# Second layer of a fused attention and two-layer kernel: y loaded a block earlier and split in place, weight conversion spaced out, weight sums kept, low parts on VectorE

## The chip, the cores and the metric

One core of a Trainium2 chip runs the whole program. The metric is device microseconds of one execution; "before" is the median of three runs. All trace numbers are from one profiled execution of the kernel before, in microseconds from its first instruction.

## What is computed

```python
# attention between x [8, 8, 512, 64] and state [8, 8, 32, 64], both ways,
# gives x of the next layer: 8 * 544 rows, 512 columns
gate = 1.0 / (1.0 + np.exp(-(x @ w_gate)))      # 512 -> 1536
y = gate * (x @ w_val) @ w_out                  # 1536 -> 512
h = y @ w_in                                    # 512 -> 2048
g = np.where(h >= 1, h, np.where(h <= -1, 0.0, (h + 1) ** 2 / 4.0))
out = g @ w_out2                                # 2048 -> 512
```

All in fp32. The kernel gets that accuracy from a faster matmul format (fp32r) by splitting every operand into a high and a low part and multiplying three times: high by high, high by low, low by high. The high part is a ScalarE copy, the low part a subtraction, raw minus high.

## The kernel before

The program is written as one order by hand: each engine executes its instructions in the order in which the code issues them, and every load and store is issued by SyncE, in that same order. The 4352 rows are nine blocks: eight (j = 0 to 7) of 512 rows, and a last one (j = 8) of 256 rows. The first layer writes its result y, block by block, to DRAM (`y_dram`).

**The block loop of the second layer's first product** (lines 1202 to 1234) has eight units per block, `n = 8 * j + m`. `emit_g2` (line 770) does one unit: 24 matmuls of 128 x 512 (`mm3`, lines 216 to 218; half as wide in the last block) into one of four PSUM tiles, then the activation in three steps: VectorE line 782, ScalarE line 785, VectorE line 786, into a tile `sg2` of three buffers. The store of that tile to `hd_dram` (line 787) is issued after the next unit has been emitted (`put`). The operand y of the next block is loaded after unit 6 of the current block by `load_y` (line 754) into two staging tiles, and split (`split`, lines 128 and 129: ScalarE y_hi, VectorE y_lo) before unit 7 is emitted. y_hi and y_lo have one tile in each of two pools, which the blocks use in turn.

Beside this, in units 0 to 23, weights are converted. `weights.slot` (line 191) advances a pipeline: load a row block of weights as raw words (`wraw`, line 146), two ScalarE steps (lines 155, 156), two VectorE steps (lines 162, 166), and then either a split (the last six tiles of w_in) or a store of the tile `ca` to `w2_dram` (line 176, 16 tiles of the second w_out). There are three buffers of `wraw` and of `ca`. The loop calls three slots in each of units 0 to 2, and two in each unit after.

**The last product** (`second`, line 865) multiplies in blocks of 2 x 2 by Strassen's scheme: seven products M1 to M7 instead of eight. Each of 36 groups of 14 steps needs seven h tiles (`hc`): `prep_h` loads four pieces of h, VectorE makes four sums (line 835), ScalarE the high parts (line 838), and the low parts (line 842) are made by VectorE and GpSimd in turn, four and three. A step is six matmuls of 256 columns, three in the last block (lines 794 to 796). The eight weight steps (w2 tiles, 0 to 7) are made by `prep_w2` (line 702): four loads from `w2_dram`, four sums on VectorE (line 727), high parts on ScalarE (735), low parts on VectorE (128 x 768) and GpSimd (128 x 1024; line 740). Steps 0 to 2 are prepared during the block loop, 3 to 7 during the first block of the last product, by a list of step numbers (`extra`):

```python
    for i in range(3, 8):
        load, *rest = prep_w2(i, w2p)
        if i < 5:
            load()
        else:
            extra.setdefault(7 * (i - 4), []).append(load)
        for n, f in enumerate(rest):
            extra.setdefault(7 * (i - 3) + n, []).append(f)
```

At the end of each block `combine` adds the seven products (line 924) and stores the output.

Of the kernel before, what the change touches and what calls it, by code (L numbers as in the profile page):

```python
# [25 lines left out]
def attention_moe_moe_kernel(  # L26
# [675 lines left out]
    def prep_w2(i, p):  # L702

        box = []

        def load():
            t = p.tile([128, 2, 7, 256], F32R, tag="w2", name="w2")
            x = wt_pool.tile([128, 256], F32, tag="wb", name="wb", bufs=2)
            box.extend((t, x))
            u = 4 * (i // 2) + i % 2  # L710
            a, b = w2_dram[u], w2_dram[u + 2]
            lo, hi = slice(0, 256), slice(256, 512)
            for n, d, c in ((0, a, lo), (1, b, lo), (2, b, hi), (None, a, hi)):
                nc.sync.dma_start(out=x if n is None else f32(t[:, 1, n]), in_=d[:, c])

        def sums():
# [4 lines left out]
            for o, a, b in (  # L721
# [5 lines left out]
                nc.vector.tensor_tensor(out=x[:, o - 3], in0=a, in1=b, op=SUB)  # L727
# [9 lines left out]
        def low(o, eng):  # L737
            src, n = part(o)
            t = box[0]
            eng.tensor_tensor(out=t[:, 1, n], in0=src, in1=f32(t[:, 0, n]), op=SUB)  # L740

        def last():
            low(False, nc.gpsimd)
            w2_t[i] = box[0]

        return [
            load,
            sums,
            lambda: high(True),
            lambda: (low(True, nc.vector), high(False)),  # L750
# [3 lines left out]
    def load_y(p, j, i, rp):  # L754
        n = S if j < B else NSB
        tag, bufs = ("hraw", 2) if rp is hr else ("io", 2)
        rv = rp.tile([128, 2, 512], F32, tag=tag, name="raw", bufs=bufs)[:, :, :n]
        nc.sync.dma_start(out=rv, in_=y_dram[j][:, 2 * i : 2 * i + 2])
        if i == 0:
            y_t[j] = (  # L760
                p.tile([128, 4, S], F32R, tag="y_hi", name="y_hi"),
                p.tile([128, 4, S], F32R, tag="y_lo", name="y_lo"),
            )
        hi, lo = y_t[j]
        o = slice(2 * i, 2 * i + 2)
        return lambda: split(hi[:, o, :n], lo[:, o, :n], rv)
# [3 lines left out]
    def emit_g2(j, m2):  # L770
# [10 lines left out]
        sg = p2.tile([128, 2, 512], F32, tag="sg2", name="sg2", bufs=3)[:, :, :n]  # L781
# [21 lines left out]
    def prep_h(q):  # L803
# [36 lines left out]
        def low(j, i):  # L840
            hi, lo = get(j)
            (nc.gpsimd if i % 2 else nc.vector).tensor_tensor(  # L842
                out=lo, in0=raw(j), in1=f32(hi), op=SUB
            )
# [441 lines left out]
```

## Time and profile before

| | us |
|---|---|
| three runs, median (lowest to highest) | 1592.81 (1589.39 to 1597.24) |
| the profiled execution | 1589.33 |
| its span, first to last instruction | 1587.2 |
| mean granted clock of TensorE, as a share of full speed | 0.969 |

The span is what the trace covers; 2.1 us of the execution's own time lie around it. In the trace, PE is TensorE, DVE is VectorE, ACT is ScalarE, POOL is GpSimd and SP is SyncE. L and a number is the line of the kernel above. Durations of neighbouring instructions on one engine overlap a little, since an instruction's end is counted when its write has been acknowledged.

### The profile page before, as it was taken

To read this page: it belongs to the slowest core of one execution; us is meant where nothing else is said; L and a number is where in the kernel's file an instruction comes from. 1 tells how busy PE (TensorE), PEld (TensorE's weight loads), DVE (VectorE), ACT (ScalarE), POOL (GpSimd) and SP (SyncE) were. 2 spreads that over 40 slices of the span, in tenths; PEclk is the share of its full clock that TensorE was granted. 3 is DMA by queue.
4 is the path that set the end of the run, shared out by engine and by line. 5 is a ranking of instruction groups with operands and counts; after the bars stand their busy time and mean duration, and the time that the engine had idled before them with its cause. 6 is when DMAs were issued, how large, how long until landed. Compare 5 with 4: busy or idle time off the path is not lost.

```text
span 1587.2 us, 28914 instructions
## 1 busy us (share of the span) xinstructions
PE 1469.1 (93%) x12176; PEld 1255.5 (79%) x12176; DVE 960.8 (61%) x1084; ACT 634.3 (40%) x896; POOL 223.2 (14%) x142
## 2 busy tenths in 40 slices
PE   7999978999899999999993999899998799999997
PEld 6677766887677777788972788677887799999997
DVE  6666455553466633441274645554455999999995
ACT  6655345433465523331253322222223444444442
POOL 2100022000000000000000000000002555545552
PEclk9999988999999999999996999999999899999999
DMA  6244455634466635754476532332345244444432
GB/s 212 95 161 168 154 207 191 200 120 153 162 230 235 232 124 195 236 198 146 145 232 224 187 117 109 132 121 106 120 146 167 72 134 134 133 134 134 133 121 80
DMA packets 140553, 249.86 MB, mean 157 GB/s; under 512 B 14729, under 2 KB 83337, under 8 KB 140425
## 3 DMA queue, kind: packets, MB, share of 16 engines
q1 hardware_dynamic: 140424, 248.03, 46.3%
q8 instruction: 95, 1.56, 0.4%
q14 instruction: 34, 0.27, 0.1%
HBM read 152.57 MB, written 95.42 MB: 156 GB/s over the span
## 4 chain that ended last, share of the span: by engine, by line
PE 70%; DVE 11%; DMA 9%; ACT 4%; issue 3%; SPq 1%; DVEq 0%; ACTq 0%
PE ps L510 17%; PE o L796 6%; PE o L794 6%; PE o L795 6%; PE ps L217 5%; PE ps L218 5%; PE ps L216 5%; PE ps L599 5%; PE ps L600 5%; PE ps L601 4%; DMA raw<-y_dram 3%; PE ps L483 3%; DMA w_dram<-ca 2%; ACT sg L785 2%; DVE cy L162 1%
## 5 line engine op out<-in xcount | busy, mean ns | idle before, releaser
L796 PE MATMUL o<-w,hc 128*128 128x256 f32 x952 | 271.1, 285 | 16.2 <-DVE hc L842 16.1
L794 PE MATMUL o<-w,hc 128*128 128x256 f32 x952 | 270.3, 284 | 2.4 <-DVE sg L786 1.7
L795 PE MATMUL o<-w,hc 128*128 128x256 f32 x952 | 269.8, 283 | 0.0
L510 PE MATMUL ps<-at_hi,M 32*128 32x512 f32 x3072 | 259.0, 398 | 3.0 <-ACT e L317 2.4
L216 PE MATMUL ps<-y_hi,wi 128*128 128x512 f32 (+1 forms) x576 | 221.3, 384 | 37.1 <-ACT y_hi L128 37.1
L217 PE MATMUL ps<-y_lo,wi 128*128 128x512 f32 (+1 forms) x576 | 221.9, 385 | 5.4 <-DVE y_lo L129 5.4
L218 PE MATMUL ps<-y_hi,wi 128*128 128x512 f32 (+1 forms) x576 | 220.6, 383 | 0.0
L796 PEld LDWEIGHTS o<-w,hc 128*128 128x128 f32 x952 | 183.2, 192 | 18.2 <-DVE hc L842 18.2
L510 PEld LDWEIGHTS ps<-at_hi,M 32*128 32x128 f32 x3072 | 151.8, 184 | 47.4 <-issue 15.3
L794 PEld LDWEIGHTS o<-w,hc 128*128 128x128 f32 x952 | 184.1, 193 | 3.3 <-issue 1.7
L795 PEld LDWEIGHTS o<-w,hc 128*128 128x128 f32 x952 | 183.1, 192 | 0.0
L785 ACT ACTIVATE sg<-sg,half 128x1024 f32<-128x1024 f32 (+1 forms) x72 | 79.6, 1105 | 233.9 <-DVE sg L782 233.9
L599 PE MATMUL ps<-oh_hi,wo 128*128 128x512 f32 x384 | 158.0, 411 | 4.0 <-ACT oh_hi L583 4.0
L600 PE MATMUL ps<-oh_lo,wo 128*128 128x512 f32 x384 | 154.0, 401 | 8.0 <-DVE oh_lo L585 7.9
L216 PEld LDWEIGHTS ps<-y_hi,wi 128*128 128x128 f32 x576 | 110.6, 192 | 59.7 <-ACT y_hi L128 38.8
L601 PE MATMUL ps<-oh_hi,wo 128*128 128x512 f32 x384 | 153.4, 400 | 3.7 <-DVE wo L187 3.7
L510 PE MATMUL ps<-at_lo,M 32*128 32x512 f32 x1536 | 156.8, 392 | 0.0
L842 POOL TENSOR_TENSOR hc<-hc 128x512 fp32r<-128x512 f32 (+1 forms) x72 | 112.0, 1555 | 301.9 <-ACT hc L838 186.7
L786 DVE TENSOR_TENSOR sg<-sg,ps 128x1024 f32<-128x1024 f32 (+1 forms) x72 | 83.7, 1162 | 96.9 <-ACT sg L785 96.9
L842 DVE TENSOR_TENSOR hc<-hs,hc 128x512 fp32r<-128x512 f32 (+1 forms) x108 | 139.4, 1332 | 0.0
L740 POOL TENSOR_TENSOR w<-wt,w 128x1024 fp32r<-128x1024 f32 x8 | 19.6, 2449 | 810.6 <-ACT w L735 810.6
L217 PEld LDWEIGHTS ps<-y_lo,wi 128*128 128x128 f32 x576 | 110.5, 192 | 28.9 <-DVE y_lo L129 8.3
(118 smaller groups left out, 2319.6 us busy)
## 6 DMA issues: line engine op xcount, KB each, us to landing
hd_dram<-sg SPq DMA_DIRECT2D x64, 512.0 KB, 2.9
h_dram<-sg SPq DMA_DIRECT2D x48, 512.0 KB, 4.4
hraw<-h_dram SPq DMA_DIRECT2D x48, 512.0 KB, 4.8
hc<-hd_dram SPq DMA_DIRECT2D x96, 256.0 KB, 4.1
wraw<-in_moe_w_out_dram SPq DMA_DIRECT2D x28, 512.0 KB, 4.0
wraw<-in_moe_w_gate_dram SPq DMA_DIRECT2D x48, 256.0 KB, 2.9
wraw<-in_moe_w_val_dram SPq DMA_DIRECT2D x48, 256.0 KB, 3.6
ws_dram<-w SPq DMA_DIRECT2D x24, 512.0 KB, 5.2
```

What stands on the lines that cost most here:

```text
L216: nc.tensor.matmul(out=ps, lhsT=wh, rhs=vh, start=(i == 0), stop=False)
L217: nc.tensor.matmul(out=ps, lhsT=wh, rhs=vl, start=False, stop=False)
L218: nc.tensor.matmul(out=ps, lhsT=wl, rhs=vh, start=False, stop=(i == n - 1))
L510: nc.tensor.matmul(out=ps[r // 2][:, r % 2], lhsT=M[o, l, e, c], rhs=a[o, e], start=(h == 0 and j == 0), stop=(h == H - 1 and j == 2),)
L599: nc.tensor.matmul(out=ps, lhsT=wh[:, c], rhs=hi, start=first, stop=False)
L600: nc.tensor.matmul(out=ps, lhsT=wh[:, c], rhs=lo, start=False, stop=False)
L601: nc.tensor.matmul(out=ps, lhsT=wl[:, c], rhs=hi, start=False, stop=last)
L785: nc.scalar.activation(out=sg, in_=sg, func=AF.Square, bias=half, scale=0.5)
L794: nc.tensor.matmul(out=ps, lhsT=wh, rhs=vh, start=start and i == 0, stop=False)
L795: nc.tensor.matmul(out=ps, lhsT=wh, rhs=vl, start=False, stop=False)
L796: nc.tensor.matmul(out=ps, lhsT=wl, rhs=vh, start=False, stop=last)
L842: (nc.gpsimd if i % 2 else nc.vector).tensor_tensor(out=lo, in0=raw(j), in1=f32(hi), op=SUB)
```

## The change

- y: `load_y` now makes both loads at once, straight into the memory of y_lo, and splits in place. The next block's y is loaded before unit 1 of the current block, and split before units 4 and 5. The staging tiles are gone, and `sg2` has two buffers instead of three.
- Conversion: from unit 3 on one slot per unit, to unit 27 instead of 23.
- Weights: four steps (0 to 3) are prepared in the block loop and stay resident. For steps 4 to 7 the four sums are also made there and kept in DRAM (`ws2_dram`); the last stage loads them (`ready`) and only splits.
- Low parts: all on VectorE, of the weights and of h.

```diff
@@ -699,32 +699,44 @@
...
-    def prep_w2(i, p):
+    ws2_dram = {i: tc.dram_tile([128, 4, 256], F32, name=f"ws2_dram_{i}") for i in range(4, 8)}
+    def prep_w2(i, p, kept=False, ready=False):
...
-            x = wt_pool.tile([128, 256], F32, tag="wb", name="wb", bufs=2)
...
-            for n, d, c in ((0, a, lo), (1, b, lo), (2, b, hi), (None, a, hi)):
-                nc.sync.dma_start(out=x if n is None else f32(t[:, 1, n]), in_=d[:, c])
+            box.append(t)
+            for n, src in enumerate((a[:, c], b[:, c], b[:, d])):
+                nc.sync.dma_start(out=f32(t[:, 1, n]), in_=src)
+            if ready:
+                box.append(f32(t[:, 1, 3:7]))
+                nc.sync.dma_start(out=box[1], in_=ws2_dram[i])
+            else:
+                x = wt_pool.tile([128, 256], F32, tag="wb", name="wb", bufs=2)
+                box.append(x)
+                nc.sync.dma_start(out=x, in_=a[:, d])
...
+        def keep():
+            nc.sync.dma_start(out=ws2_dram[i], in_=box[1])
...
@@ -734,36 +746,38 @@
...
-        def low(o, eng):
+        def low(o):
             src, n = part(o)
             t = box[0]
-            eng.tensor_tensor(out=t[:, 1, n], in0=src, in1=f32(t[:, 0, n]), op=SUB)
+            nc.vector.tensor_tensor(out=t[:, 1, n], in0=src, in1=f32(t[:, 0, n]), op=SUB)
         def last():
-            low(False, nc.gpsimd)
+            low(False)
             w2_t[i] = box[0]
-        return [
-            load,
-            sums,
+        if kept:
+            return [load, sums, keep]
+        return [load] + [sums] * (not ready) + [
             lambda: high(True),
-            lambda: (low(True, nc.vector), high(False)),
+            lambda: (low(True), high(False)),
             last,
         ]
...
-    def load_y(p, j, i, rp):
+    def load_y(p, j):
         n = S if j < B else NSB
-        tag, bufs = ("hraw", 2) if rp is hr else ("io", 2)
-        rv = rp.tile([128, 2, 512], F32, tag=tag, name="raw", bufs=bufs)[:, :, :n]
-        nc.sync.dma_start(out=rv, in_=y_dram[j][:, 2 * i : 2 * i + 2])
-        if i == 0:
-            y_t[j] = (
-                p.tile([128, 4, S], F32R, tag="y_hi", name="y_hi"),
-                p.tile([128, 4, S], F32R, tag="y_lo", name="y_lo"),
-            )
-        hi, lo = y_t[j]
-        o = slice(2 * i, 2 * i + 2)
-        return lambda: split(hi[:, o, :n], lo[:, o, :n], rv)
...
+        hi, lo = y_t[j] = (
+            p.tile([128, 4, S], F32R, tag="y_hi", name="y_hi"),
+            p.tile([128, 4, S], F32R, tag="y_lo", name="y_lo"),
+        )
+        def step(i):
+            o = slice(2 * i, 2 * i + 2)
+            raw = f32(lo[:, o, :n])
+            nc.sync.dma_start(out=raw, in_=y_dram[j][:, o])
+            return lambda: split(hi[:, o, :n], lo[:, o, :n], raw)
+        return [step(i) for i in range(2)]
...
@@ -778,7 +792,7 @@
...
-        sg = p2.tile([128, 2, 512], F32, tag="sg2", name="sg2", bufs=3)[:, :, :n]
+        sg = p2.tile([128, 2, 512], F32, tag="sg2", name="sg2", bufs=2)[:, :, :n]
...
-        def low(j, i):
+        def low(j):
             hi, lo = get(j)
-            (nc.gpsimd if i % 2 else nc.vector).tensor_tensor(
-                out=lo, in0=raw(j), in1=f32(hi), op=SUB
-            )
+            nc.vector.tensor_tensor(out=lo, in0=raw(j), in1=f32(hi), op=SUB)
...
@@ -1180,7 +1192,7 @@
...
-            ys = [load_y(pa, 0, c, hr) for c in range(2)]
+            ys = load_y(pa, 0)
...
@@ -1202,24 +1214,28 @@
...
-            if m == 7:
-                while ys:
-                    ys.pop(0)()
+            if m == 1 and j < B:
+                ys = load_y(yb if j % 2 == 0 else pa, j + 1)
+            if m in (4, 5) and j < B:
+                ys.pop(0)()
             then = emit_g2(j, m)
             if put:
                 put()
             put = then
-            if n < 24 and not weights.empty():
-                for _ in range(3 if n < 3 else 2):
+            if n < 28 and not weights.empty():
+                for _ in range(3 if n < 3 else 1):
                     weights.slot()
-            if n == 24:
+            if n == 28:
                 assert weights.empty()
                 st_conv.close()
-                w2p = pool("w2a", side="right", bufs=3)
+                w2p = pool("w2a", side="right", bufs=4)
                 wt_pool = pool("wt", side="right")
-                todo2 += [f for i in range(3) for f in prep_w2(i, w2p)]
+                todo2 += [f for i in range(4, 8) for f in prep_w2(i, w2p, kept=True)]
+                todo2 += [f for i in range(4) for f in prep_w2(i, w2p)]
             elif todo2 and n < 8 * B - 8:
-                todo2.pop(0)()
+                for f in todo2[: 2 if n % 3 == 0 else 1]:
+                    f()
+                del todo2[: 2 if n % 3 == 0 else 1]
...
-            if m == 6 and j < B:
-                ys = [load_y(yb if j % 2 == 0 else pa, j + 1, c, p2) for c in range(2)]
...
@@ -1238,19 +1252,19 @@
...
-    w2p = pool("w2b", stack=st_o, bufs=5)
+    w2p = pool("w2b", stack=st_o, bufs=4)
...
-    for i in range(3, 8):
-        load, *rest = prep_w2(i, w2p)
-        if i < 5:
+    for i in range(4, 8):
+        load, *rest = prep_w2(i, w2p, ready=True)
+        if i < 6:
             load()
         else:
-            extra.setdefault(7 * (i - 4), []).append(load)
+            extra.setdefault(7 * (i - 5), []).append(load)
         for n, f in enumerate(rest):
-            extra.setdefault(7 * (i - 3) + n, []).append(f)
+            extra.setdefault(7 * (i - 4) + 4 + n, []).append(f)
```

What the two orders look like at three places follows.

SyncE in block 0. Before, the second y (`y_dram_108`) is loaded here, behind unit 5's result (`hd_dram_116` is block 0's result, `w_dram_...` the converted rows of the second w_out, `ca` their source):

```order
L787 DMA hd_dram_116<-sg_9994 128x1024
L146 DMA wraw<-in_moe_w_out_dram 128x1024
L176 DMA w_dram_131<-ca 128x512
L146 DMA wraw<-in_moe_w_out_dram 128x1024
L176 DMA w_dram_132<-ca 128x512
L758 DMA raw<-y_dram_108 128x1024 x2
L787 DMA hd_dram_116<-sg_10042 128x1024
```

Now, from the block's first weight loads on:

```order
L146 DMA wraw<-in_moe_w_in_dram 128x4x256 x4
L777 DMA y_lo<-y_dram_108 128x1024 x2
L801 DMA hd_dram_116<-sg_9721 128x1024
L146 DMA wraw<-in_moe_w_in_dram 128x4x256 x2
L146 DMA wraw<-in_moe_w_out_dram 128x1024
L801 DMA hd_dram_116<-sg_9772 128x1024
L146 DMA wraw<-in_moe_w_out_dram 128x1024 x3
L801 DMA hd_dram_116<-sg_9838 128x1024
L146 DMA wraw<-in_moe_w_out_dram 128x1024
L176 DMA w_dram_125<-ca 128x512
L801 DMA hd_dram_116<-sg_9904 128x1024
```

The load has moved ahead of the block's first result and of all stores of `ca`, and there is one load and one store of weight rows per unit where there were two.

VectorE at the start of the last stage, before (`hs` are sums of h tiles, `hc` low parts, `wt` sums of weights, `w_...` low parts of weights), from the last activation step on:

```order
L786 TENSOR_TENSOR sg_12233<-sg_12233,ps_12208 128x2x256
L727 TENSOR_TENSOR wt<-wb,w_12257 128x256
L727 TENSOR_TENSOR wt<-w_12257,wt 128x256
L727 TENSOR_TENSOR wt<-w_12257,wb 128x256
L727 TENSOR_TENSOR wt<-w_12257,wt 128x256
L835 TENSOR_TENSOR hs_12293<-ht,hc 128x512
L835 TENSOR_TENSOR hs_12303<-hs_12293,hc 128x512
L835 TENSOR_TENSOR hs_12305<-hc,ht 128x512
L740 TENSOR_TENSOR w_12257<-w_12257 128x768
L835 TENSOR_TENSOR hs_12316<-hc,hs_12303 128x512
L842 TENSOR_TENSOR hc<-hc 128x512
L842 TENSOR_TENSOR hc<-hs_12303,hc 128x512
```

and now:

```order
L800 TENSOR_TENSOR sg_12282<-sg_12282,ps_12257 128x2x256
L849 TENSOR_TENSOR hs_12335<-ht,hc 128x512
L849 TENSOR_TENSOR hs_12344<-hs_12335,hc 128x512
L849 TENSOR_TENSOR hs_12346<-hc,ht 128x512
L849 TENSOR_TENSOR hs_12355<-hc,hs_12344 128x512
L856 TENSOR_TENSOR hc<-hc 128x512 x2
L752 TENSOR_TENSOR w_12306<-w_12306 128x768
L856 TENSOR_TENSOR hc<-hs_12344,hc 128x512
L752 TENSOR_TENSOR w_12306<-w_12306 128x1024
L856 TENSOR_TENSOR hc<-hc 128x512
```

The weight sums are gone, the weight's first low part stands behind two low parts of h instead of ahead of them, and the low parts that GpSimd made stand in VectorE's list.

SyncE at the same place, before, behind the last result:

```order
L714 DMA w_12257<-w_dram_130 128x256
L714 DMA w_12257<-w_dram_132 128x256 x2
L714 DMA wb<-w_dram_130 128x256
L714 DMA w_12263<-w_dram_133 128x256
L714 DMA w_12263<-w_dram_135 128x256 x2
L714 DMA wb<-w_dram_133 128x256
L824 DMA hc<-hd_dram_116 128x2x256
L828 DMA ht<-hd_dram_116 128x2x256
L824 DMA hc<-hd_dram_116 128x2x256 x2
```

and now:

```order
L716 DMA w_12306<-w_dram_133 128x256
L716 DMA w_12306<-w_dram_135 128x256 x2
L719 DMA w_12306<-ws_dram_141 128x1024
L716 DMA w_12311<-w_dram_134 128x256
L716 DMA w_12311<-w_dram_136 128x256 x2
L719 DMA w_12311<-ws_dram_142 128x1024
L838 DMA hc<-hd_dram_116 128x2x256
L842 DMA ht<-hd_dram_116 128x2x256
L838 DMA hc<-hd_dram_116 128x2x256 x2
```

The last load of each weight step is four times as large, and still ahead of the h tiles.

## Rows read from the trace of the kernel before

**Rows 1.** The page: busy time and share of the span, by engine.
```profile
PE 1469.1 (93%) x12176; PEld 1255.5 (79%) x12176; DVE 960.8 (61%) x1084; ACT 634.3 (40%) x896; POOL 223.2 (14%) x142
```

**Rows 2.** Busy time by stage: stretch, length, engines (count), clock, DMA share, GB/s.
```profile
785.70:1212.40 426.70, 383.62 (x1729) 317.17 (x1729) 235.77 (x233) 132.97 (x150) 11.07 (x6) 0.94 0.42 146
1212.40:1576.80 364.40, 346.47 (x2856) 343.63 (x2856) 328.14 (x367) 151.15 (x265) 178.43 (x110) 0.99 0.40 128
```

**Rows 3.** TensorE's waits, 785.7 to 1212.4: us in total, times, longest.
```profile
PE ps L216 <- ACT y_hi L128: 37.1, 4, 28.7
PE ps L217 <- DVE y_lo L129: 5.4, 7, 2.2
```

**Rows 4.** Timeline of TensorE at the first border: start, us, [idle before <- releaser].
```profile
858.21 0.80 PE L216 MATMUL ps<-y_hi,wi 128*128 128x512 f32 x1 [28.66 <-ACT y_hi L128]
```

**Rows 5.** Timeline of SyncE's issues in block 0.
```profile
790.58 7.43 SPq L146 DMA_DIRECT2D wraw<-in_moe_w_in_dram  x4
...
850.07 0.97 SPq L758 DMA_DIRECT2D raw<-y_dram  x2
```

**Rows 6.** All waits, 785.7 to 860: the one of ScalarE on stores.
```profile
ACT ca L155 <- DMA w_dram<-ca: 21.3, 7, 5.4
```

**Rows 7.** Timeline of VectorE in the block loop.
```profile
823.23 1.22 DVE L782 TENSOR_SCALAR sg<-ps 128x1024 f32<-128x1024 f32 x1
...
932.19 1.22 DVE L782 TENSOR_SCALAR sg<-ps 128x1024 f32<-128x1024 f32 x1 [1.77 <-PE ps L218]
934.63 1.22 DVE L786 TENSOR_TENSOR sg<-sg,ps 128x1024 f32<-128x1024 f32 x1 [1.22 <-ACT sg L785]
937.63 1.23 DVE L782 TENSOR_SCALAR sg<-ps 128x1024 f32<-128x1024 f32 x1 [1.77 <-PE ps L218]
```

**Rows 8.** Timeline of ScalarE: first copy of two neighbouring output blocks.
```profile
1312.65 0.60 ACT L944 ACTIVATE cm<-o 128x512 f32<-128x512 f32 x1 [0.89 <-PE o L796]
...
1352.49 0.60 ACT L944 ACTIVATE cm<-o 128x512 f32<-128x512 f32 x1 [0.92 <-PE o L796]
```

**Rows 9.** Busy time by stretch, just after the first border.
```profile
860.00:862.00 2.00, 2.00 (x6) 1.55 (x5) 1.80 (x2) 0.17 (x1) 0.00 (x0) 0.50 0.00 0
```

**Rows 10.** TensorE's waits, 1212.4 to 1576.8.
```profile
PE o L796 <- DVE hc L842: 16.1, 7, 6.1
```

**Rows 11.** Timeline of TensorE, start of the last stage.
```profile
1230.45 0.58 PE L796 MATMUL o<-w,hc 128*128 128x256 f32 x1 [6.14 <-DVE hc L842]
...
1236.17 0.33 PE L795 MATMUL o<-w,hc 128*128 128x256 f32 x1
```

**Rows 12.** The page's DMA issues: count, KB each, median us to landing.
```profile
hd_dram<-sg SPq DMA_DIRECT2D x64, 512.0 KB, 2.9
```

**Rows 13.** Groups by form, 1212 to 1590: busy us, mean ns.
```profile
L842 DVE TENSOR_TENSOR hc<-hs,hc 128x512 fp32r<-128x512 f32 x93 | 126.9, 1406 | 0.0
```

**Rows 14.** Timeline of VectorE, and of GpSimd: low parts.
```profile
1197.74 1.80 DVE L842 TENSOR_TENSOR hc<-hs,hc 128x512 fp32r<-128x512 f32 x1
...
1209.50 0.69 DVE L842 TENSOR_TENSOR hc<-hs,hc 128x512 fp32r<-128x512 f32 x1
...
1197.70 1.29 POOL L842 TENSOR_TENSOR hc<-hc 128x512 fp32r<-128x512 f32 x1 [4.59 <-ACT hc L838]
```

**Rows 15.** Busy time by stretch, middle of the last stage.
```profile
1320.00:1360.00 40.00, 40.00 (x340) 40.00 (x339) 37.02 (x41) 16.97 (x29) 20.01 (x12) 1.00 0.41 135
```

**Rows 16.** Timeline of VectorE, start of the last stage.
```profile
1225.23 0.69 DVE L835 TENSOR_TENSOR hs<-ht,hc 128x512 f32<-128x512 f32 x1 [4.79 <-DMA hc<-hd_dram]
...
1226.56 1.76 DVE L835 TENSOR_TENSOR hs<-hc,ht 128x512 f32<-128x512 f32 x1
...
1229.71 0.68 DVE L842 TENSOR_TENSOR hc<-hc 128x512 fp32r<-128x512 f32 x1
```

**Rows 17.** Busy time by stretch, start of the last stage.
```profile
1216.00:1228.00 12.00, 8.30 (x70) 8.11 (x68) 4.26 (x7) 4.32 (x6) 4.14 (x2) 1.00 0.91 282
1226.00:1270.00 44.00, 30.29 (x204) 28.68 (x205) 43.76 (x46) 18.76 (x29) 24.72 (x14) 0.88 0.31 96
```

More of the change, by code (lines that the diff above doesn't have):

```diff
@@ L700, in attention_moe_moe_kernel @@
     w2_t = {}
-    def prep_w2(i, p):
+    ws2_dram = {i: tc.dram_tile([128, 4, 256], F32, name=f"ws2_dram_{i}") for i in range(4, 8)}
+    def prep_w2(i, p, kept=False, ready=False):
         box = []
+        u = 4 * (i // 2) + i % 2
+        a, b = w2_dram[u], w2_dram[u + 2]
+        c, d = slice(0, 256), slice(256, 512)
         def load():
             t = p.tile([128, 2, 7, 256], F32R, tag="w2", name="w2")
-            x = wt_pool.tile([128, 256], F32, tag="wb", name="wb", bufs=2)
[L709 to L712, printed above, removed]
-            for n, d, c in ((0, a, lo), (1, b, lo), (2, b, hi), (None, a, hi)):
-                nc.sync.dma_start(out=x if n is None else f32(t[:, 1, n]), in_=d[:, c])
+            box.append(t)
[8 more added lines that the diff above has]
+                nc.sync.dma_start(out=x, in_=a[:, d])
         def sums():
@@ L720, in sums @@
             b11, b21, b22 = (f32(t[:, 1, n]) for n in range(3))
-            for o, a, b in (
+            for o, l, r in (
                 (M5, b12, b11),
@@ L726, in sums @@
             ):
-                nc.vector.tensor_tensor(out=x[:, o - 3], in0=a, in1=b, op=SUB)
+                nc.vector.tensor_tensor(out=x[:, o - 3], in0=l, in1=r, op=SUB)
+        def keep():
+            nc.sync.dma_start(out=ws2_dram[i], in_=box[1])
         def part(o):
@@ L861, in prep_h @@
             S.setdefault(2 + i, []).append(lambda j=j: high(j))
-            S.setdefault(3 + i, []).append(lambda j=j, i=i: low(j, i))
+            S.setdefault(3 + i, []).append(lambda j=j: low(j))
         return S
```

## Prediction

> **What bounds the kernel now.** TensorE is busy 93% of the span [rows 1], so I look for the places where it is not. The table of stages [rows 2] splits the part that the change touches: the block loop of the second layer's first product (785.7 to 1212.4 us, 426.7 long, TensorE busy 383.6) and the last product (1212.4 to 1576.8, 364.4 long, busy 346.5). Before 785.7 the change alters nothing but where the first y lands. The table of waits gives what TensorE waited for in the block loop: only the split of the next y, 37.1 us for y_hi and 5.4 for y_lo, eleven waits [rows 3], all at block borders. The first alone is 28.66 us and ends at 858.21 [rows 4].
>
> Why the first is so long: the loads of the second y are issued at 850.07 [rows 5], behind SyncE's stores of w_out rows, and those come late because ScalarE, which also stands in the chain of each unit, waited 21.3 us for earlier stores of `ca` to land [rows 6]. At the other borders the load is issued so late that its landing and the split still follow when TensorE is through.
>
> How long would the loop be without waits? One unit (24 matmuls) takes 5.44 us: VectorE's first steps of two neighbouring units start at 932.19 and 937.63 [rows 7]. 64 units are 348.2 us. In the last block a matmul has 256 columns, as in the last stage, where 336 of them take 39.84 us (the first copy of two neighbouring output blocks, 1312.65 and 1352.49 [rows 8]), 0.1186 each: 8 x 24 x 0.1186 = 22.8. Together 371.0 of 426.7, so 55.7 us are lost. The listed waits are 42.5; the other 13.2 are mostly matmuls at half clock after a wait: from 860 to 862 the granted clock is 0.50, that is 1.2 GHz, and six matmuls start in 2 us [rows 9], where 5.44 us hold 24 at full clock.
>
> The last stage: 2856 matmuls of 0.1186 us are 338.6 of 364.4, so 25.8 are lost. The listed waits are for VectorE's low parts, 16.1 us in seven [rows 10]. The longest, 6.14, ends at 1230.45 [rows 11].
>
> **The change, part by part.**
>
> *y a block ahead.* The load moves from behind unit 6 to before unit 1; the order rows show it directly behind the four w_in loads, with no `ca` store ahead of it. In the profiled run SyncE is through those at 798 [rows 5], so it lands well before the splits at units 4 and 5 (from about 807). In later blocks the two loads stand behind the store of the unit that read their tiles last, so they add no wait for what is queued behind them. All the waits and their half-clock stretches should go: minus 55.7. The split itself costs the same in place. No engine takes over as the bound: a unit's chain on VectorE and ScalarE is 1.22 + 1.22 + 1.22 = 3.66 us (932.19 to 934.63, plus the last step [rows 7]) of 5.44.
>
> *What is late next* is the evacuation in block 0, which has nine conversion slots in its first three units, now as before. At unit 4 VectorE starts at 823.23 [rows 7]; TensorE had ended that unit at 785.7 + 5 x 5.44 = 812.9, so evacuation is 10.3 us behind. With four PSUM tiles TensorE can stand 3 x 5.44 - 3.66 = 12.7. With one slot a unit instead of two, and a split step of 1.2 us in units 4 and 5, I get 10.9 at worst and then a recovery of about 0.5 a unit. That is close, so I charge 1 us; bounds 0 and 5 (two slots more than counted, 1.3 us of VectorE each, in both units).
>
> *sg2 from three buffers to two.* A result must be stored before the unit after next starts its evacuation: 3.7 + landing 2.9 [rows 12] against 10.9, free. In the last block, with units of 2.85, it is a chain of 2.1, issue 0.4 and at most that landing, 5.4 against 5.7: thin, so 0.5 us charged, up to 3 if stores land late. The loop gains 55.7 - 1.5 = **54.2** (50 to 55.7).
>
> *Conversion spaced out, kept sums, fourth resident step.* This work moves within or into the block loop. VectorE and ScalarE are busy 235.8 and 133.0 of its 426.7 us, DMA 42% [rows 2]; five more weight loads of 512 KB, four stores of 512 KB and some 20 us of VectorE come on top, spread over 27 units. I cost it at nothing; if that cover fails, the PSUM margin above pays first.
>
> *Last stage.* Steps 3 to 7 no longer compute sums there, and GpSimd no longer works. What that does to VectorE: the low part takes 1406 ns on average over 93 [rows 13], but one that starts beside GpSimd's takes 1.80 and one of the same form with GpSimd idle 0.69 [rows 14]. So VectorE loses time whenever GpSimd runs. It is busy 37.0 of 40 us now [rows 15]. Afterwards a block has 44 sums and low parts and 8 adds, at most 52 x 0.69 = 35.9 us against 39.84: it fits, even with the 12 low parts that move in.
>
> The Trainium skill has a rule against this part: the page "Perfetto Trace Analysis", section "Optimizing Scalar/DVE Operations", says that with a saturated DVE it may make sense to offload work to Scalar or even GpSimd, and adds that DVE and GpSimd share a port, so that between those two it might not help. By the plain rule the sum would be rival 3's, 1564; by the rows it is 1521. The 1.80 against 0.69 agrees with what it adds.
>
> Then the first wait of that stage. TensorE ended its first 14 steps at 1230.45 - 6.14 = 1224.3. VectorE started on the next group at 1225.23, when the h tiles had landed, and reached the first low part at 1229.71 [rows 16]: a sum of 1.76 ran beside GpSimd, and a weight's low part stood ahead. Afterwards it is four sums and a low part, 4 x 0.61 + 0.69 (one follows the other every 0.6 to 0.7), 3.1 and 0.1 to start. But the loads of two weight steps ahead of the h tiles grow by 2 x 384 KB; at the 282 GB/s of that stretch [rows 17] that is 2.8 us if all of it comes first, 0 if none of it does; between these I take the middle, 1.4, since loads in flight share the engines. TensorE resumes at 1225.2 + 1.4 + 3.2 = 1229.8: 5.5 idle instead of 6.1. Half clock follows again, from 1230.45 to 1236.17 now [rows 11], 2.9 lost. The rest of the 25.8, 16.8 us, is 10.0 in the other waits for low parts, and half clock and short gaps around them; as VectorE then runs ahead, I keep 1.8 of it (the opening of the stage and its end). Loss 5.5 + 2.9 + 1.8 = 10.2 instead of 25.8: **15.6 us gained** (11 to 18).
>
> **Sum.** The profiled execution took 1589.33 us (span 1587.2 and 2.1 around it). Minus 54.2 and 15.6 is 1519.5. It lay 3.5 us under the median of the runs shown, 1592.81, at the low end of their range; I carry half of that over: **1521**. Its own range is 1511 to 1530.
>
> **Rivals.**
> 1. *The last stage starts as it did*: the larger weight loads hold the h tiles back by the full 2.8 us, and the waits after the first were for landings. Against: from 1226 to 1270 VectorE is busy 43.76 of 44 us [rows 17], so it was the late one. The stage then gains little, 1521 + 11 to 15: 1532 to 1536.
> 2. *Part of the first border's wait stays*: evacuation falls more than 12.7 us behind in block 0, or SyncE reaches the load late. For: 10.3 already. Against: its place in the queue. Up to 28.7 come back: 1526 to 1550.
> 3. *VectorE becomes the bound of the last stage*: its 37.0 us of 40 are all work of its own, and 12 x 0.69 = 8.3 come on top: 45.2 against 39.84, 5.4 a block, 43 over eight: 1564. Against: 1.80 and 0.69 for one form.
> 4. *Slower than before*: 1406 ns is VectorE's price of a low part by its operands, not by GpSimd. 28 x 1.406 + 24 x 0.69 = 55.9 us a block, 16.1 over, 129 over eight: 1650. It decides from 1.15 us a low part (48.8 a block, 9 over, eats the gain of both stages). For: the mean of 93. Against: 0.69 at 1209.50.
>
> **How the numbers follow.** Forecast 0.71, rival 1 0.12, rival 2 0.09, rival 3 0.04, rival 4 0.03, no change that can be measured 0.01. About 0.5% (8 us) is what a measurement of this kernel can tell from no change. All but the last two lie further down than that, 0.96; I say 0.95 faster, 0.02 same, 0.03 slower. The range 1510 to 1541 takes in the forecast with the bounds of its terms, rival 1, and half of rival 2.
>
> **What would show it.** Right: no wait of TensorE on y_hi or y_lo in the loop; the loop near 373 us at granted clock 1.00; the second y's loads issued near 798; VectorE's low parts all near 0.69; a block of the last stage still 39.84; one wait of 4 to 8 us some 12 us into that stage and no series after it. Wrong: TensorE waiting for an sg step around units 6 to 10; low parts over 1 us with GpSimd idle; blocks over 40 us; a series of waits after the first in the last stage.

## Result, and the profile after

The changed kernel takes 1527.65 us (median of four runs, 1525.03 to 1528.74), beside 1593.06 of the kernel before in the same comparison: ratio 0.9586, 95% interval 0.9559 to 0.9613. The forecast of 1521 was 6.6 us low and had the time inside its range. The profiled execution took 1528.28 us (span 1526.5, mean granted clock 0.977).

The page's busy time by engine of the changed kernel, which answers to [rows 1]:

```profile
PE 1460.4 (96%) x12176; PEld 1255.3 (82%) x12176; DVE 908.4 (60%) x1200; ACT 628.6 (41%) x896; POOL 33.7 (2%) x26
```

Busy time by stage (columns as in [rows 2]); the block loop now runs from 792.0 to 1169.8 and the last stage to 1515.7:

```profile
792.00:1169.80 377.80, 373.46 (x1730) 312.38 (x1730) 239.79 (x260) 133.39 (x152) 0.00 (x0) 1.00 0.52 177
1169.80:1515.70 345.90, 339.62 (x2855) 338.82 (x2854) 271.10 (x454) 145.16 (x263) 0.00 (x0) 0.99 0.43 138
```

Against [rows 2] the loop is 48.9 us shorter. The last stage, cut in the same way, took 364.0 before (the row there reaches 0.4 further) and is 18.1 shorter. Before the loop the code is the same, yet that part took 792.0 us instead of 785.7; over the 13 executions profiled here it took between 785.7 and 792.1, and in the execution that the prediction was summed on it was the shortest of all.

TensorE's waits from 792 to the end, which answer to [rows 3] and [rows 10]:

```profile
PE ps L216 <- DVE sg L800: 3.8, 1, 3.8
PE o L810 <- DVE hc L856: 3.6, 1, 3.6
PE o L808 <- DVE sg L800: 1.6, 1, 1.6
PE o L808 <- ACT hc L852: 1.0, 1, 1.0
PE ps L217 <- DVE y_lo L129: 0.5, 1, 0.5
```

The 42.5 us of waits for the split of y have shrunk to 0.5, and the series for low parts (16.1 in seven) to 3.6 in one, with 1.0 just before it for a high part. New is the first row, a wait for a step of the activation (the evacuation of a PSUM tile), in unit 14. The third row stood in the kernel before too, 1.7 in two waits. The y load that [rows 5] show at 850.07 is now issued 12.8 us after the loop's start (timeline of SyncE):

```profile
797.15 7.53 SPq L146 DMA_DIRECT2D wraw<-in_moe_w_in_dram  x4
804.79 0.91 SPq L777 DMA_DIRECT2D y_lo<-y_dram  x2
```

The low parts among the groups by form, which answer to [rows 13]:

```profile
L856 DVE TENSOR_TENSOR hc<-hs,hc 128x512 fp32r<-128x512 f32 x124 | 81.0, 687 | 1.3 <-ACT hc L852 1.2
```

Busy time of a stretch in the middle of the last stage, as in [rows 15]:

```profile
1300.00:1340.00 40.00, 40.00 (x342) 40.00 (x341) 31.91 (x53) 16.52 (x29) 0.00 (x0) 1.00 0.40 133
```

The first copies of two neighbouring output blocks on ScalarE's timeline, as in [rows 8]:

```profile
1294.08 0.60 ACT L956 ACTIVATE cm<-o 128x512 f32<-128x512 f32 x1 [1.33 <-PE o L810]
1333.64 0.60 ACT L956 ACTIVATE cm<-o 128x512 f32<-128x512 f32 x1 [1.69 <-PE o L810]
```

A low part takes 687 ns instead of 1406; VectorE does 53 instructions in 31.9 of 40 us where it did 41 in 37.0; a block takes 39.56 us instead of 39.84.

**Where the loop still loses.** Timeline of VectorE, SyncE and TensorE (PE) around the second border:

```profile
854.47 1.22 DVE L800 TENSOR_TENSOR sg<-sg,ps 128x1024 f32<-128x1024 f32 x1 [1.22 <-ACT sg L799]
...
857.58 2.08 SPq L777 DMA_DIRECT2D y_lo<-y_dram  x2
859.70 0.43 SPq L801 DMA_DIRECT2D hd_dram<-sg  x1
...
868.45 1.23 DVE L796 TENSOR_SCALAR sg<-ps 128x1024 f32<-128x1024 f32 x1 [6.53 <-DMA hd_dram<-sg]
...
872.26 0.77 PE L216 MATMUL ps<-y_hi,wi 128*128 128x512 f32 x1 [3.80 <-DVE sg L800]
```

The stretch behind that wait (busy time, clock):

```profile
872.00:880.00 8.00, 7.74 (x27) 6.28 (x28) 5.30 (x8) 3.34 (x4) 0.00 (x0) 0.79 0.69 199
```

Unit 8's result is ready at 855.7. Its store is issued at 859.70, 4.0 us later; for the last 2.1 of them SyncE issues the third block's y loads (1 MB). The store lands just before 868.45, 8.7 us after its issue. With two sg2 buffers unit 10 needs that one, and its evacuation waits 6.53 us. TensorE has 12.7 us of slack for that, but evacuation was still 10.1 us behind (TensorE ended unit 10 at 792.0 + 11 x 5.44 = 851.8, VectorE could have begun at 861.9). Unit 10 starts 16.6 us after TensorE was through with it (868.45 - 851.8), so 16.6 - 12.7 = 3.9 comes through to TensorE: the 3.80 of unit 14, which needs unit 10's PSUM tile.

The kernel before already had such a store, issued at 851.08 right behind the two y loads of [rows 5]. The DMA issues of a window of its trace that holds this store alone (851.1 to 851.3):

```profile
hd_dram<-sg SPq DMA_DIRECT2D x1, 512.0 KB, 8.5
```

And of the six stores of block 0 ahead of it (785.7 to 849):

```profile
hd_dram<-sg SPq DMA_DIRECT2D x6, 512.0 KB, 6.4
```

The median of 2.9 over all 64 stores [rows 12] holds for neither place.

### The profile page after: what moved, and what is told of

The parts are those of the page before. It is cut to its first block, busy times and chain, and to the rows that moved or that the text cites. A ratio compares the mean times of both kernels' runs of the same rounds, so it can differ in the third digit from the quotient of the medians.

```text
span 1526.5 us, 28851 instructions
## 1 busy us (share of the span) xinstructions
PE 1460.4 (96%) x12176; PEld 1255.3 (82%) x12176; DVE 908.4 (60%) x1200; ACT 628.6 (41%) x896; POOL 33.7 (2%) x26
## 4 chain that ended last, share of the span: by engine, by line
PE 86%; DVE 4%; DMA 4%; ACT 3%; SPq 1%; issue 1%; DVEq 0%; ACTq 0%
PE ps L510 18%; PE ps L216 8%; PE ps L218 8%; PE ps L217 8%; PE o L810 7%; PE o L809 7%; PE o L808 7%; PE ps L599 5%; PE ps L600 5%; PE ps L601 5%; PE ps L483 3%; PE ps L293 2%; DVE cy L162 1%; DMA hd_dram<-sg 1%; PE ps L278 1%
## 5 line engine op out<-in xcount | busy, mean ns | idle before, releaser
L216 PE MATMUL ps<-y_hi,wi 128*128 128x512 f32 (+1 forms) x576 | 218.4, 379 | 3.8 <-DVE sg L800 3.8
L217 PE MATMUL ps<-y_lo,wi 128*128 128x512 f32 (+1 forms) x576 | 218.0, 378 | 0.5 <-DVE y_lo L129 0.5
L218 PE MATMUL ps<-y_hi,wi 128*128 128x512 f32 (+1 forms) x576 | 217.9, 378 | 0.0
L216 PEld LDWEIGHTS ps<-y_hi,wi 128*128 128x128 f32 x576 | 108.8, 189 | 24.4 <-issue 4.4
L218 PEld LDWEIGHTS ps<-y_hi,wi 128*128 128x128 f32 x576 | 108.7, 189 | 20.2
L494 DVE TENSOR_TENSOR M<-ps,M 128x1024 fp32r<-128x1024 f32 x48 | 58.7, 1224 | 101.1 <-ACT M L488 98.3
L852 ACT ACTIVATE hc<-hc 128x512 fp32r<-128x512 f32 (+1 forms) x108 | 64.8, 602 | 129.3 <-DMA hc<-hd_dram 122.7
```

Of the source, the lines that this page charges most:

```text
L216: nc.tensor.matmul(out=ps, lhsT=wh, rhs=vh, start=(i == 0), stop=False)
L217: nc.tensor.matmul(out=ps, lhsT=wh, rhs=vl, start=False, stop=False)
L218: nc.tensor.matmul(out=ps, lhsT=wl, rhs=vh, start=False, stop=(i == n - 1))
```

## The experiments

All ratios are to the kernel before, run beside each on the same chip, with 95% intervals. "Loop" and "last stage" are cut as above; the expectations of runs 1, 3 and 5 and the first of 4 were made with another cut, the changed kernel's as 380.3 and 343.8. The intervals of runs 1 to 3 overlap with the changed kernel's (0.9559 to 0.9613), so there the stages and the waits carry the reading.

**1. A third sg2 buffer**, given back before unit 28, when its memory is wanted for weights.

```diff
-        sg = p2.tile([128, 2, 512], F32, tag="sg2", name="sg2", bufs=2)[:, :, :n]
+        u = 8 * j + m2
+        third = u % 3 == 2 and u < 27
+        sg = (sgx if third else p2).tile(
+            [128, 2, 512], F32, tag="sg2", name="sg2", bufs=1 if third else 2
+        )[:, :, :n]
```

> The changed kernel with a third sg2 buffer for units 0 to 26 (it lies in a pool that closes before the h tiles need the room). Theory: the changed kernel's block loop (380.3 us, 371 without waits) loses its 8 to 9 us because VectorE waits 6.5 us for the store of unit 8 to free one of two sg2 buffers; with three the loop is 371 to 375 us, no wait of VectorE on that store is over 1 us and TensorE does not wait for an sg step: 1519 to 1523 in all. Rival: the backlog of the nine conversion slots in units 0 to 2 stalls TensorE by itself; then the loop stays at 378 to 381 and TensorE still waits 3 to 4 us near unit 14.

1521.10 us, ratio 0.9543 (0.9517 to 0.9569); loop 371.9, last stage 346.0. Busy time of the loop:

```profile
786.40:1158.30 371.90, 371.64 (x1729) 311.38 (x1729) 239.44 (x260) 133.50 (x152) 0.00 (x0) 1.00 0.52 180
```

TensorE no longer waits for sg in the loop, and VectorE's waits for stores, 9.3 us in four with two buffers, are down to one:

```profile
DVE sg L800 <- DMA hd_dram<-sg: 0.4, 1, 0.4
```

5.9 us of the loop are thus the price of two buffers with the y loads ahead of the store. The loop repeats well enough for that: it took 376.9 to 378.2 in the three versions that keep both (the change, runs 3 and 5) and 371.9 to 373.2 in the five that give up one of them (runs 1, 2, both of 4, and 10).

**2. The y loads one place later on SyncE**, two buffers kept:

```diff
-            if m == 1 and j < B:
-                ys = load_y(yb if j % 2 == 0 else pa, j + 1)
...
             if put:
                 put()
             put = then
+            if m == 1 and j < B:
+                ys = load_y(yb if j % 2 == 0 else pa, j + 1)
```

> The changed kernel, with the y loads of a block issued one place later on SyncE: behind the store of the unit before instead of ahead of it. Two sg2 buffers stay. Theory (the store of unit 8 landed 8.6 us after its issue because 1 MB of y loads had been issued just ahead of it): that store lands in 3 to 5 us, the waits of 3.8 us on sg and 6.5 us on the store go, loop 371.5 to 373.5, total 1521 to 1523. Rival (the store is slow because of the weight loads of that time, wherever y stands): loop 377 to 379, unchanged.

1521.13 us, ratio 0.9543 (0.9516 to 0.9569); loop 372.5. Timeline of SyncE and VectorE at the same border:

```profile
852.88 0.45 SPq L801 DMA_DIRECT2D hd_dram<-sg  x1
853.43 2.16 SPq L777 DMA_DIRECT2D y_lo<-y_dram  x2
857.75 0.68 SPq L801 DMA_DIRECT2D hd_dram<-sg  x1
...
858.08 1.22 DVE L796 TENSOR_SCALAR sg<-ps 128x1024 f32<-128x1024 f32 x1 [0.52 <-DMA hd_dram<-sg]
...
864.88 1.22 DVE L796 TENSOR_SCALAR sg<-ps 128x1024 f32<-128x1024 f32 x1 [1.80 <-DMA hd_dram<-sg]
```

Unit 8's store now lands 5.2 us after its issue (852.88 to 858.08) and unit 9's, behind the y loads, 7.1. The expected 3 to 5 us was too good: the six stores of this run between 815 and 850, with no y loads near them, took 5.1 in the median, so unit 8's is no longer late for its block. Each delay is now within TensorE's slack, and its wait is gone as with a third buffer.

**3. h tiles ahead of weight steps 4 and 5** at the start of the last stage:

```diff
-        if i < 6:
-            load()
-        else:
-            extra.setdefault(7 * (i - 5), []).append(load)
+        extra.setdefault(7 * max(i - 5, 0) + (i == 5), []).append(load)
```

> The changed kernel, with the loads of weight steps 4 and 5 issued behind the four h tile loads at the start of the last stage instead of ahead of them. Theory: the wait there (3.6 and 1.0 us, then some 2.5 lost at half clock) comes from h tiles that land behind 1.8 MB of weights; with the h tiles first, VectorE begins on them 3 to 5 us sooner, TensorE waits under 1 us and the last stage goes from 343.8 to 336 to 339 us: 1521 to 1524. Rival: the wait only moves, since now the weight's high and low parts stand in the two engines' queues ahead of later h low parts and wait for their own landing: TensorE waits a little later, stage 341 to 345 us, time unchanged.

1521.81 us, ratio 0.9545 (0.9523 to 0.9567); last stage 341.4 instead of 345.9. That is 4.5 us less, where the theory had 4.8 to 7.8 and the rival at most 2.8; the time is inside the theory's. Two rows of TensorE's timeline at its start:

```profile
1181.41 0.38 PE L810 MATMUL o<-w,hc 128*128 128x256 f32 x1 [0.39 <-DVE hc L856]
1183.15 0.39 PE L810 MATMUL o<-w,hc 128*128 128x256 f32 x1 [0.77 <-DVE hc L856]
```

Busy time and clock of the stretch around them:

```profile
1180.00:1190.00 10.00, 8.85 (x74) 8.45 (x73) 9.31 (x13) 6.80 (x12) 0.00 (x0) 1.00 1.02 354
```

The changed kernel at the same place, TensorE's timeline:

```profile
1187.02 0.58 PE L810 MATMUL o<-w,hc 128*128 128x256 f32 x1 [3.60 <-DVE hc L856]
```

And its busy time and clock from there:

```profile
1187.00:1195.00 8.00, 7.98 (x45) 7.98 (x46) 8.00 (x11) 5.37 (x9) 0.00 (x0) 0.63 0.55 189
```

So the weight loads ahead did hold the h tiles back. VectorE's first sum of h tiles starts 14.0 us into the stage with the change (1183.74 - 1169.8), 8.7 with the h tiles first (1176.06 - 1167.3), and 12.8 in the kernel before (1225.23 - 1212.4 [rows 16]). The loads ahead cost 5.2 of these, and with the larger ones it is about 1.2 more than before, where the prediction charged 1.4. What is left are four waits under 0.8 us for VectorE, after which the clock stays at 1.00; after 3.60 us the granted clock is 0.63, which over 8 us is 3.0 us lost.

**4. Edits 1 and 3 together, and 2 and 3 together.**

> Both edits together. Theory: they are independent, loop 371 to 375 and last stage 336 to 339 us: 1512 to 1517 us, 0.8 to 1.0% faster than the changed kernel. Rival: one of the two does nothing, 1519 to 1523.

1514.12 us, ratio 0.9495 (0.9475 to 0.9515); loop 372.4, last stage 342.0.

> The changed kernel with two short edits: the y loads of a block one place later on SyncE, behind the store of the unit before; and at the start of the last stage the loads of weight steps 4 and 5 behind the first four loads of h tiles. Two sg2 buffers stay. Theory (the two edits act in different stages and add up, and the order of the y loads does as much as a third sg2 buffer): loop 371.5 to 373.5, last stage 341 to 343, total 1513 to 1516, the same as with the third buffer. Rival (without the third buffer another unit waits): loop 375 to 379, total 1517 to 1522.

1515.10 us, ratio 0.9511 (0.9480 to 0.9542); loop 373.2, last stage 341.1. The loops and totals are as expected, and so is the second stage; the first is 3.9 us shorter where 4.8 to 7.8 were expected, as in run 3. The edits add up, and both versions beat the changed kernel; the second does it with two moved loads and no memory.

**5. Low parts back on GpSimd**, all else as changed:

```diff
-            nc.vector.tensor_tensor(out=lo, in0=raw(j), in1=f32(hi), op=SUB)
+            (nc.gpsimd if i % 2 else nc.vector).tensor_tensor(
+                out=lo, in0=raw(j), in1=f32(hi), op=SUB
+            )
...
-            low(False)
+            low(False, nc.gpsimd)
```

> The changed kernel with the low parts divided between VectorE and GpSimd as before. Theory: VectorE is held up while GpSimd runs, so its low parts take 1.4 us on average again and it is busy over 90% of a block; a block of the last stage is 39.84 instead of 39.57 us, and the first block has several waits again, fewer than before since the weight sums are gone: last stage 350 to 356 us instead of 343.8, 1535 to 1541 in all. Rival: the sums were what overloaded VectorE, not the sharing; then the stage is 344 to 347.

1538.36 us, ratio 0.9641 (0.9614 to 0.9668); last stage 358.7. VectorE's low parts and sums in the groups by form:

```profile
L856 DVE TENSOR_TENSOR hc<-hs,hc 128x512 fp32r<-128x512 f32 x93 | 128.9, 1431 | 0.0
L849 DVE TENSOR_TENSOR hs<-hc,ht 128x512 f32<-128x512 f32 x31 | 55.4, 1787 | 0.0
```

Busy time in the middle of the stage:

```profile
1300.00:1340.00 40.00, 40.00 (x342) 40.00 (x341) 37.80 (x40) 17.36 (x30) 19.63 (x12) 1.00 0.40 132
```

TensorE's wait for low parts in the stage:

```profile
PE o L810 <- DVE hc L856: 10.9, 5, 6.9
```

The same form that takes 687 ns takes 1431 with GpSimd at work: 40 instructions fill 37.8 us where 53 took 31.9. The stage is 12.8 us longer, just over the expected 6 to 12, and nearly all of it at its start; the blocks after the first stay at 39.56 to 39.67, since VectorE still fits. My 39.84 for the block was a miss: its shortening does not come from GpSimd.

**6. The kernel before with the low parts alone moved** (the same lines the other way round):

> The kernel before, with one part of the change alone: all low parts of the last stage's operands on VectorE, none on GpSimd. Theory (GpSimd slows VectorE, so taking its work away gives VectorE time back): loop 426 unchanged, last stage 350 to 355 instead of 364, low parts near 0.69 us each, total 1579 to 1585. Rival 3 or 4 of the prediction (VectorE becomes the bound, or 1.4 us is its own price): last stage 380 or more, total over 1600. Block of the last stage: 39.84 if its 39.57 after the change comes from something else, 39.57 if it comes from GpSimd's absence.

1577.65 us, ratio 0.9893 (0.9874 to 0.9913); last stage 354.7, loop 422.0; TensorE's waits in the loop and in the last stage:

```profile
PE ps L216 <- ACT y_hi L128: 35.8, 4, 29.0
...
PE o L796 <- DVE hc L842: 10.5, 6, 5.8
```

The low parts by form:

```profile
L842 DVE TENSOR_TENSOR hc<-hs,hc 128x512 fp32r<-128x512 f32 x124 | 80.8, 683 | 1.2 <-ACT hc L838 1.1
```

683 ns in the old kernel too. The low parts alone give 9.3 of the last stage's 18.1 us (364.0 to 354.7), the weights alone 5.3 (to 358.7, run 5), the two together 3.5 more. Of the 5.3, 2.4 are the shorter block (8.5 x 0.28), which stays at 39.84 here; the kept sums and the fourth resident step were not tried apart. The loop's 4.7 us less was not expected and puts the total 1.4 under its range; of it the listed waits (40.1 instead of 42.5) hold 2.4.

**7. The kernel before with the early y alone** (`load_y` and its calls as changed; three buffers and two slots a unit stay):

> The kernel before, with one part of the change alone: y loaded a block ahead and split in place; three sg2 buffers and two conversion slots per unit stay as they were, and so does the last stage. Theory (the early load removes the waits at all nine borders, but with two slots a unit the evacuation in block 0 falls more than 12.7 us behind, so that spacing is needed too): loop 390 to 398 us with waits of TensorE on VectorE's sg steps of 15 to 20 us together in blocks 0 and 1, last stage 364 as before, total 1557 to 1565. Rival (spacing is not needed): loop 371 to 378, total 1538 to 1545.

1570.09 us, ratio 0.9849 (0.9828 to 0.9869); loop 402.6, last stage 364.1. All waits in the loop, TensorE's for sg and y_hi and ScalarE's for stores of `ca`:

```profile
PE ps L216 <- DVE sg L788: 15.8, 6, 5.0
PE ps L216 <- ACT y_hi L128: 4.6, 1, 4.6
...
ACT ca L155 <- DMA w_dram<-ca: 37.6, 11, 5.6
```

The waits for y gave way to waits for PSUM. Only 4.6 us for y are left, but 15.8 for evacuation came in their place. The total missed the expected span (1557 to 1565) by 5, and the loop its own by 4.6, the size of that one wait for y_hi, which I had not counted.

**8. The changed kernel with two slots a unit again** (`3 if n < 3 else 2`).

> The changed kernel, with two conversion slots per unit again from unit 3 on; y early, two sg2 buffers and all else as changed. Theory (the spacing is needed once y no longer stalls TensorE): the evacuation falls some 30 us behind by unit 10, TensorE waits 15 to 20 us for PSUM in blocks 0 and 1, loop 393 to 402. Rival (spacing does nothing, the engines catch up anyway): loop 377 to 380.

1551.79 us, ratio 0.9729 (0.9714 to 0.9743); loop 401.6. The same three rows of its waits:

```profile
PE ps L216 <- DVE sg L800: 15.6, 6, 4.7
PE ps L216 <- ACT y_hi L128: 4.4, 1, 4.4
...
ACT ca L155 <- DMA w_dram<-ca: 37.5, 10, 5.5
```

Loop and waits are as the theory had them, and run 7's almost to the digit, with two buffers instead of three. ScalarE, which stands in every unit's chain, waits up to 5.5 us at a time for a store of `ca`; with one slot a unit these waits are 11.9 us in nine, none over 2.0.

**9. The changed kernel with the late y** (loaded in place behind unit 6, split before unit 7), conversion spaced out.

> The changed kernel, with y loaded late again (in place, behind unit 6, split before unit 7); conversion stays spaced out, two sg2 buffers and all else as changed. Theory (each of the two parts alone leaves about half of the loop's loss: SyncE reaches the late load only when unit 5 has been evacuated, some 12 us behind TensorE in block 0): the first border's wait falls from 28.7 to 15 to 22 us, the later borders keep 10 to 14 together, with half clock behind each; loop 405 to 418 us, total 1553 to 1567. Rival A (the late load alone is the loss, spacing does nothing for it): first wait 27 or more, loop 422 to 428. Rival B (spacing alone was enough): loop below 390.

1572.01 us, ratio 0.9854 (0.9820 to 0.9889); loop 422.1, four over the theory's and at rival A's lower edge, and the total five over. TensorE's timeline at the first border:

```profile
852.93 0.79 PE L216 MATMUL ps<-y_hi,wi 128*128 128x512 f32 x1 [16.97 <-ACT y_hi L128]
```

All waits of TensorE in the loop:

```profile
PE ps L216 <- ACT y_hi L128: 35.3, 5, 17.0
PE ps L217 <- DVE y_lo L129: 3.8, 7, 0.8
```

The first wait fell from 28.66 [rows 4] to 16.97, as the theory has it and against rival A, but the next ones grew to 8.6 and 7.2, so that the sum (39.1) is nearly the old 42.5. The loop by both parts, in us (the two of the old kernel with three sg2 buffers):

| | two slots a unit | one slot a unit |
|---|---|---|
| y late | 426.7 (before) | 422.1 (run 9) |
| y a block ahead | 402.6 (run 7), 401.6 (run 8) | 377.8 (the change) |

Spacing is worth 24 us with the early y; the early y 24 with two slots and 44 with one. Neither has a price of its own. With the late y spacing shows 4.6, no more than the loop of run 6 differs (4.7) with y and the slots as before, so there it may be worth nothing.

**10. Resident weight steps in another order**, on top of edits 2 and 3, to see where the shorter block comes from:

```diff
-                todo2 += [f for i in range(4) for f in prep_w2(i, w2p)]
+                todo2 += [f for i in (3, 2, 1, 0) for f in prep_w2(i, w2p)]
```

> The kernel with the two short edits (y loads behind the store, h tiles ahead of weight step 4), with the four resident weight steps prepared in the order 3, 2, 1, 0 instead of 0, 1, 2, 3, so that step 3 takes the place in memory that step 0 had, and step 0 the one that step 3 had. What each would make of the mean distance of matmuls in the last stage, 113 ns in steps 3 and 4 now, 117 in 5 and 6, 120 in the others: if it goes with the weights' place in memory, step 0 comes down to 113 and step 3 goes up to 120; if it goes with the step's place in the program (what else runs beside it), step 3 stays at 113 and step 0 at 120. A block of the last stage is 39.57 us in both cases, the total 1513 to 1520.

1513.84 us in its one execution. The expectation numbers the steps one too high: it counts the last step of a block (7) as 0 of the next. Counted from the first matmul of the stage, 42 to a step, the steps at 113 ns are 2 and 3, both resident, and 4 and 5 are those that it has at 117. The test still holds, since step 3 takes the place of step 0 and step 2 that of step 1. Busy time by stretch, steps 7 and 0 and then most of 2 and 3:

```profile
1242.00:1250.00 8.00, 8.00 (x69) 8.00 (x68) 7.83 (x14) 2.67 (x5) 0.00 (x0) 1.00 0.69 242
1255.00:1263.00 8.00, 8.00 (x73) 8.00 (x72) 6.80 (x11) 3.35 (x6) 0.00 (x0) 1.00 0.27 81
```

69 and 73 matmuls in 8 us, the same counts as with the old order. Steps 2 and 3 keep their 113 ns and steps 0 and 1 their 120. The speed does not follow the place of the resident weights among each other in memory.

## Why the prediction was right, and where it was off

The span was predicted as 1587.2 - 54.2 - 15.6 = 1517.4 and came as 1526.5. The 9.1 us are 6.3 of the part ahead of the loop, 5.3 of the loop (377.8 against 426.7 - 54.2 = 372.5), 2.9 the other way in the last stage (345.9 against 348.8), and 0.4 from where the two stages were cut. How the 6.6 us by which the median was missed split between the first part and the loop is open, since only one of the four executions has a trace.

- *y a block ahead: right.* Issued 12.8 us into the loop, as expected; one wait of 0.5 us on y is left of eleven. Run 7 shows it is not enough alone.
- *What is late next: right in kind and in size.* Evacuation was 12.1 us behind at unit 5 (VectorE at 836.76, TensorE through at 792.0 + 6 x 5.44 = 824.6), where I had 10.9 against a limit of 12.7. It reached TensorE in no unit of block 0, and recovered by about 0.4 a unit (10.1 at unit 10) where I had 0.5. The sign of being wrong that I named, a wait for an sg step around units 6 to 10, came in unit 14 and was for unit 10's step. That the spacing is needed stood in that step and not in rival 2; runs 7 and 8 show that two slots a unit bring 15.6 to 15.8 us of waits.
- *sg2 from three buffers to two: the step that failed.* "3.7 + landing 2.9 against 10.9, free" took the median landing, and nothing for the store's place in SyncE's queue. For unit 8 they were 8.7 and 4.0, so 16.4 in all. The trace of the kernel before had 8.5 for the store behind its y loads, and 3.7 + 8.5 = 12.2 against 10.9 would not have been free. That the moved loads "add no wait for what is queued behind them" was the same error: the store behind them waited 2.1 us for their issue alone. I looked for the thin spot in the last block; it was at the second border, where the moved y loads meet a unit whose evacuation had not caught up. With the slower clock behind the wait (granted 0.79 on average from 872 to 880) it cost 5.9 us by run 1, which has a third buffer, where I had charged 0.5, with 3 as its upper bound.
- *Conversion, kept sums, fourth step cost nothing: right.* With the buffer's price gone the loop takes 371.9, against 371.0 for units alone, at 52% DMA share.
- *Last stage: right.* Of 345.9 us, 8.5 blocks of 39.56 are 336.3, so 9.6 are lost (10.2 predicted): 6.2 in the listed waits, 3.0 at the lower clock (granted 0.63 over 8 us). The first wait came as 1.0 and 3.6 (predicted 5.5), 13 us into the stage. The 2.9 us gained beyond the forecast are mostly the shorter blocks, 8.5 x 0.28 = 2.4, which nothing in the prediction foresaw: luck, and it hid almost half of the 5.3 by which the loop was missed.
- *VectorE and GpSimd: right, and the part the forecast hung on.* 687 ns for all low parts, 1431 with GpSimd back. Rivals 3 and 4 fall. The advice that the Trainium skill gives in "Perfetto Trace Analysis", section "Optimizing Scalar/DVE Operations", to offload a saturated VectorE to GpSimd would have cost 12.8 us here (run 5). Its own reservation, that the two share a port and such a move might not help, agrees with 687 against 1431 ns; no run here shows the port itself.
- *Rival 1* had its mechanism right and its size wrong: the weight loads do hold the h tiles back, but the larger ones add about 1.2 us and not 2.8, and the waits after the first were VectorE's and went. Run 3 gains 4.5 us by turning the order round.

## What to carry to other kernels

When a change takes buffers away and moves a load, follow the store that frees a buffer through its queue at the place where the moved load passes it, and price it there with a landing that the old trace shows behind such a load, not with the median. When a stall goes, ask which engine had used it to catch up: here the early load was worth 24 us without the spacing and 44 with it. Where an engine is slowed by another that shares its work, taking over all of it can leave that engine less busy (here 31.9 us of 40 instead of 37.0): compare one instruction's time beside the other engine with its time alone.

## What was not expected of the hardware

- In the last stage a matmul of 256 columns follows the one before after 113, 118 or 120 ns at a granted clock of 1.00 (means over the 42 starts of one weight step in the timeline), depending on the step: 113 in step 2 before, in steps 2 and 3 after. That one step makes the block 0.28 us shorter (42 x 6.6 ns). TensorE's timeline, the first matmuls of steps 3 and 4 of a block, before and after (5.04 us apart, then 4.76):

```profile
1331.60 0.28 PE L794 MATMUL o<-w,hc 128*128 128x256 f32 x1
...
1336.64 0.28 PE L794 MATMUL o<-w,hc 128*128 128x256 f32 x1
```

```profile
1273.46 0.28 PE L808 MATMUL o<-w,hc 128*128 128x256 f32 x1
...
1278.22 0.28 PE L808 MATMUL o<-w,hc 128*128 128x256 f32 x1
```

  Step 3 is the one that the change made resident, so its weights moved from pool `w2b` to `w2a`. In the seven blocks between the first and the last, in all 13 traces, the speed goes with the pair of pools that hold a step's weights and its h tiles (`hcp0` for steps 0, 1, 4 and 5, `hcp1` for the others). In ns:

| weights in | h tiles in `hcp0` | h tiles in `hcp1` |
|---|---|---|
| `w2a` (resident) | 120 | 113 |
| `w2b` (loaded in the stage) | 118 | 120 |

  It is not GpSimd (run 5) and not the order of the weights within `w2a` (run 10). The pair is not all of it: in the half-size last block step 5 runs at 113 in nine traces and at 118 in four. No run moved a pool by itself, so the cause stays open. At 113 throughout, the stage's 2856 matmuls would take 323 us instead of 336.
- A 512 KB store issued right behind 1 MB of loads took 8.7 us to land, and 8.5 in the kernel before, where the page's median for these stores is 2.9.
- Code that no edit touches took 785.7 to 792.1 us, as much as several of the effects measured here. Stage by stage the traces repeat much better: the last stage of the five kernels with the changed kernel's last stage took 345.9, 346.0, 346.6, 346.8 and 347.7.
